# Eight chunks of q and k: rearranged in DRAM and turned in 32x32 blocks on VectorE instead of on TensorE

## The chip, the cores and the metric

The kernel runs on one core of a Trainium2 chip. A core has a TensorE (PE; its weight loads are listed as PEld), a VectorE (DVE), a ScalarE (ACT), a GpSimd (POOL) and a SyncE (SP), which here only issues transfers. Sixteen DMA engines move data between DRAM and the on-chip memory. The engines run side by side and wait for each other by semaphores; each one executes its own instructions in order. The metric is the device time of one execution in microseconds. The profile is of one execution.

## The reference

The program has two parts. The first is linear attention with a decay per head, over 4 sequences (b) of 768 tokens, 8 heads and a head size of 64:

```python
intra = np.einsum('bhic,bhjc->bhij', qb, kb) * Dmask[None]
intra = np.einsum('bhij,bhjd->bhid', intra, vb)
inter = np.einsum('bhid,bhde->bhie', qb * lam_pow[None], kv_state)
out[:, :, sl] = intra + inter
kb_dec = kb * rev_pow[None]
kv_state = lam_block[None, :, None, None] * kv_state + np.einsum('bhsd,bhse->bhde', kb_dec, vb)
```

Its output, seen as 3072 tokens by 512 features, is the x of the second part, a dense mixture of four experts (512 to 1024 to 512):

```python
for e in range(E):
    h = np.maximum(x @ w1[e], 0.0)
    out += p[:, e:e + 1] * (h @ w2[e])
```

Everything is float32.

## The kernel before, in words

**Attention.** The tokens are cut into 24 chunks of 128: chunk n is chunk c = n mod 6 of sequence b = n div 6. A chunk goes through `load` (line 111), `turn` (457), `scores` (480) and `values` (498). `load` brings q, k and v from DRAM into one tile each, with the 128 tokens on the partitions; q and k take two transfers each (for the two halves of the heads), v takes one. `turn` transposes q and k on PE with an identity matrix: four 128x128 transposes each, into the PSUM tiles `qp` and `kp` (line 463). ACT copies those into the tiles `qT` and `kT` (468 and 469), in which the two halves of the head features of a head pair lie on the partitions and the tokens run along the free dimension. For every chunk but the first of a sequence VectorE makes `qs`, q times its decay. For every chunk but the last of a sequence POOL multiplies k, in its untransposed tile, by its decay in place; the transposes read that tile before. `scores` makes the products of k and q (line 486) and has VectorE mask them; `values` makes the outputs and the state, which ACT copies into `xT`.

**Experts.** Eight chunks make a group of 1024 tokens, and there are three groups (g). The x of a group meets four experts in turn; one group with one expert is a unit, and the main loop (line 1193) runs over the twelve units, counted by `at`. Each of the two matrix products of a unit is done by Strassen's scheme with seven products (M1 to M7), and the first one is split by it once more, so its operands are sums of blocks. Those sums are made ahead of time, mostly on POOL, stored to DRAM (`w1_ops`, `x_ops`, `w2_sums`), and loaded again just before use: `feed` (line 659) loads `xs_in` and `ws_in`, one product of the first kind ahead, with two buffers each; `feed2` (764) loads the weights `w2t`, two products ahead. Before the main loop, the first group's product with the first expert is done directly (`direct_product`, line 1045), while the attention of the first group ends.

**The order of the work.** The program is written out by hand: each engine executes in the order in which the code emits. The main loop works on one unit's second product and on the next unit's first product side by side. For each of the seven products (`i`) it has eight slots (`x`), each with a few matmuls of one or of both kinds. Between them it puts:

- `rest()`, which takes one item from a list called `background`: a VectorE operation, for instance a sum for the second product or the masks of `scores`. `soon` puts an attention item at the front of that list.
- steps of the next group's attention: each chunk has three (turn, scores, and values with the load of the chunk two ahead), put in at x = 5, and for i = 1, 3, 5 at x = 2 as well, from the second unit on (line 1258). So a unit takes up to ten steps. Chunks 8 to 15 belong to the units 0 to 2, and chunks 16 to 23 begin in the unit with `at` = 3.
- `pump`, which emits the chores of POOL (the sums for later units, in a first-in first-out list) and the stores of finished sums.

All loads and stores of the main loop go through SP's queue (L123 for q and k, L667 and L669 for `feed`, L775 for `feed2`, L175 to L177 and L248 for stores). An issue there can wait for a buffer to come free, for the data that it stores, or for an earlier transfer, and everything behind it on SP then waits too.

Of the kernel before, what the change touches and what calls it, by code (L numbers as in the profile page):

```python
# [12 lines left out]
ALU = mybir.AluOpType  # L13
# [9 lines left out]
def kernel(  # L23
# [70 lines left out]
    def tt(eng, o, a, b, op):  # L94
        eng.tensor_tensor(out=o, in0=a, in1=b, op=op)  # L95
        if eng is nc.gpsimd:
            busy[0] = max(busy[0], now[0]) + math.prod(o.shape[1:]) / 480
# [13 lines left out]
    def load(n, names="qkv"):  # L111

        b, c = divmod(n, NCH)
        for name in names:
            x = small(f"{name}n")
            src = {"q": q, "k": k, "v": v}[name][b, :, c * C:(c + 1) * C, :]
            if name == "v":
                nc.sync.dma_start(out=x[:].rearrange("p (h d) -> p h d", d=D), in_=src.rearrange("h p d -> p h d"))
            else:
                to, of = x[:].rearrange("p (i r d) -> p i r d", r=2, d=D), src.rearrange("(r i) p d -> p i r d", r=2)  # L120
                for r in range(2):
                    by = nc.scalar if n < 2 and r == 1 else nc.sync
                    by.dma_start(out=to[:, :, r], in_=of[:, :, r])  # L123
            nat[n, name] = x[:].rearrange("p (h d) -> p h d", d=D)
# [219 lines left out]
    def sum_w1(e, name, a, b, op):  # L344
# [6 lines left out]
            tt(nc.gpsimd, to[c], w1_now[e][a][c], w1_now[e][b][c], op)  # L351
        w1_now[e][name] = to

    lam_bc = consts.tile([P, H], FP32, name="lam_bc")
    nc.scalar.dma_start(out=lam_bc[:], in_=lam.partition_broadcast(P))
    for n, names in ((0, "qk"), (1, "qk"), (0, "v"), (2, "qk"), (1, "v"), (3, "qk")):
# [94 lines left out]
    def soon(n, *work):  # L451

        background[0:0] = work
        if n < CPG:
            rest(len(work))

    def turn(n, tags):
        qn, kn = nat.pop((n, "q")), nat[n, "k"]
        qp = bank(tags[0], "qp")
        kp = bank(tags[1], "kp")  # L460
        for x, y in ((qp, qn), (kp, kn)):
            for ac in range(NHP):
                nc.tensor.transpose(  # L463
                    out=x[:, ac * C:(ac + 1) * C], in_=y[:, 2 * ac:2 * ac + 2].rearrange("p r d -> p (r d)"),
                    identity=ident[:],
                )
        qT, kT, qs = small("qT"), small("kT"), None
        nc.scalar.copy(out=qT[:], in_=qp[:])
        nc.scalar.copy(out=kT[:], in_=kp[:])
        if n % NCH:  # L470
            qs = small("qs")
            soon(n, lambda: tt(nc.vector, qs[:], qT[:], q_decay[:].rearrange("p h c -> p (h c)"), ALU.mult))
        turned[n] = qT, kT, qs
        if n % NCH < NCH - 1:

            kd = kn.rearrange("p (ac r) d -> p ac r d", r=2)
            by = k_decay.rearrange("p r ac -> p ac r").unsqueeze(3)
            tt(nc.gpsimd, kd, kd, by.to_broadcast([P, NHP, 2, D]), ALU.mult)

    def scores(n, tags):  # L480
        qT, kT, _ = turned[n]

        sp = [bank(tags[r], "sp") for r in range(2)]
        for ac in range(NHP):
            for r in range(2):
                nc.tensor.matmul(  # L486
                    out=sp[r][:, ac * C:(ac + 1) * C], lhsT=hc(kT)[half[r], ac], rhs=hc(qT)[half[r], ac],
                    start=True, stop=True,
                )
        st = [small("st") for _ in range(2)]  # L490
# [50 lines left out]
    def attention(g):  # L541

        steps = []
        early, late = prepare_x(g)
        for n in range(g * CPG, (g + 1) * CPG):
            steps.append(lambda n=n: turn(n, ("s0", "s1")))
            steps.append(lambda n=n: scores(n, ("s0", "s1")))

            def end(n=n):
                if n == g * CPG:  # L550
                    for m in MS:
                        until(("x", g - 1, m))
# [596 lines left out]
    def sum_own(name, a, b, op=ALU.subtract):  # L1149
# [4 lines left out]
        lambda: own_weights("M1"), sum_own("S1", "A21", "A22", ALU.add), *w2_steps[0:4], mine["M1"], *w2_steps[4:],  # L1154
        raw["A12"],
    ))
    for m in SEQ0[2:]:
        if m == SEQ0[-1]:
            for _ in range(2):
                feed2(*fill2.pop(0))  # L1160
        work = direct_product(0, m, blocks, ("g1", "g3", "q01", "q02", "q11", "q12")) if m != "M5" else [m5[1], *m5[3:]]
        for x, f in enumerate(work):
            f()
            rest()
            if x < len(work) - 1:
                now[0] += 1
                pump(0.75)

    start, w1_steps = now[0], prepare_w1(2)

# [22 lines left out]
    for at, (g, e) in enumerate(units):  # L1193
        if at == 0:
            chores.extend(prepare_w2(2) + prepare_w1(3) + prepare_w2(3) + prepare_w1(0))
        ahead = units[at + 1] if at + 1 < len(units) else None
        nested, nests = g == LAST, ahead and ahead[0] == LAST
        if g == LAST - 1:
            if e == 0:
                chores.append(turn_gates)  # L1200
            chores.extend(prepare_w2_ops(e))
        if ahead and ahead[1] == 0:
            assert not steps
            steps = attention(ahead[0] + 1) if ahead[0] + 1 < NG else []
        blocks, banks = {}, {}
        for i in range(7):
            if fill2:
                feed2(*fill2.pop(0))
            if nested or (nests and i == 6):
                for _ in range(2 if ahead else 16 if i == 0 else 4 if i > 1 else 0):  # L1210
                    if fill3:
                        feed3(*fill3.pop(0))
            if nests and i == 2:
                nc.scalar.dma_start(
                    out=gate_bc, in_=gate_rows[:, ahead[1]].partition_broadcast(P),
                )
            if nested:
                b = nested_product(e, SEQ3[i], (("q01", "q02"), ("q11", "q12"), ("g1", "g3"))[i % (2 if ahead else 3)])
                if i < 6 and (e, SEQ3[i + 1]) != PLAIN:
                    inner_sums(e, SEQ3[i + 1])  # L1220
            else:
                b = second_product(g, e, SEQ2[i], banks)
            if nests and i == 6:
                inner_sums(ahead[1], SEQ3[0], nested)
                if ahead[1] == EARLY[0]:
                    inner_sums(*EARLY, True)
            a = []
            if ahead:
                a = first_product(*ahead, SEQ[i], blocks, ("g1", "g3"))
            if not ahead:  # L1230
                order = [[], b[0:2], [], b[2:4], [], b[4:6], [], b[6:8]]
            elif nested:
                order = [b[0:2], a[0:2], b[2:4], a[2:4], b[4:6], a[4:6], b[6:8], a[6:8]]
            else:
                order = [b[0:1], a[0:2], b[1:2], a[2:4], b[2:3], a[4:6], b[3:5], a[6:8]]
            turned_back = list(after_last.get(SEQ3[i], ())) if nested and not ahead else []
            for x, part in enumerate(order):
                for f in part:
                    if f:
                        f()  # L1240
                now[0] += 1
                if joins:
                    joined()
                elif ahead or x % 2 == 0 and x + i:
                    rest()
                if nested or nests:
                    take(aside)
                if nested and ahead and x in (1, 3) and fill3:
                    feed3(*fill3.pop(0))
                if turned_back and x > 0:  # L1250
                    y = turned_back.pop(0)
                    if y:
# [40 lines left out]
```

## Time and profile before

| | |
|---|---|
| time, median of 9 runs | 1198.38 us (1196.45 to 1199.70) |
| the profiled execution's own time | 1198.89 us |
| its span, first to last instruction | 1197.1 us |
| granted TensorE clock | 1.00 |
| DMA packets | 227991, 317.94 MB |
| DMA packets under 512 B | 91680 |

The profiled execution lasted 1.8 us longer than its span. A line such as `L463` is a line of the kernel; the many sums and products made by the helper `tt` all carry L95. In a group of instructions the form is: line, engine, operation, out<-in by the program's names, partitions x elements, how many; then the busy time in us, the mean of one in ns, and after a second bar the idle time of the engine just before them with what ended it. A wait line reads: engine and line, what it waited for, then the total in us, how often, and the longest. In a timeline the first two numbers are start and duration in us; idle time before is in brackets. In a table of stretches each engine has its busy time in us and its number of instructions, in the order PE, PEld, DVE, ACT, POOL; then come the granted clock, the share of the time in which the 16 DMA engines were busy, and GB/s.

### The profile page before, as it was taken

The page shows a single profiled execution, that of the slowest core. Times are in us where ns is not written, and L with a number is a line of the kernel's source. Part 1 is how long each engine was busy: PE and PEld are TensorE (multiplying, and loading weights), DVE is VectorE, ACT ScalarE, POOL GpSimd, SP SyncE. Part 2 cuts the span into 40 slices and gives each one's busy share as a digit, 9 for nine tenths or more (in the row PEclk, how much of TensorE's full clock was granted, in tenths as well). Part 3 has the DMA queues.
Part 4 walks back from the last instruction along what each step waited for, and adds up shares of the span by engine and source line. Part 5 has one row for each costly group of instructions (what it writes and reads, how often), then busy time and mean ns, then how long its engine had stood idle before and what let it go on. Part 6 is the DMA issues. An engine that isn't in the chain of part 4 may idle for free.

```text
span 1197.1 us, 17886 instructions
## 1 busy us (share of the span) xinstructions
PE 1186.7 (99%) x6623; PEld 1029.9 (86%) x6623; DVE 790.4 (66%) x1318; ACT 261.6 (22%) x478; POOL 635.0 (53%) x600
## 2 busy tenths in 40 slices
PE   9999999999999999999999999999999999999998
PEld 8887888888888888888888888888888888888877
DVE  5597785567467656746754774774665677776784
ACT  3322122112112201311221120120142241240232
POOL 1875248359366800044434745316684683783884
PEclk9999999999999999999999999999999999999999
DMA  9885679999999985689977989898986657566542
GB/s 217 221 295 195 224 261 309 361 318 321 367 344 306 334 274 178 220 287 282 284 275 235 318 298 315 280 313 299 314 285 241 250 193 279 193 251 228 211 167 80
DMA packets 227991, 317.94 MB, mean 266 GB/s; under 512 B 91680, under 2 KB 169408, under 8 KB 227904
## 3 DMA queue, kind: packets, MB, share of 16 engines
q1 hardware_dynamic: 218352, 314.11, 77.5%
q10 hardware_dynamic: 9552, 2.69, 1.1%
q8 instruction: 52, 0.85, 0.3%
q14 instruction: 35, 0.29, 0.1%
HBM read 231.40 MB, written 85.34 MB: 265 GB/s over the span
## 4 chain that ended last, share of the span: by engine, by line
PE 91%; DVE 4%; DMA 2%; POOL 1%; SPq 1%; issue 1%; ACT 0%; ACTq 0%; DVEq 0%; POOLq 0%
PE pg L740 38%; PE q L794 32%; PE pq L966 12%; DVE m L95 2%; PE op L514 2%; PE sp L486 2%; PE pM L1058 1%; PE op L509 1%; PE kp L463 1%; DVE hS L95 1%; SPq L123 1%; PE qp L463 1%; PE op L522 1%; DMA w2b<-in_moe_w_dram 1%; PE pM L936 1%
## 5 line engine op out<-in xcount | busy, mean ns | idle before, releaser
L740 PE MATMUL pg<-xs_in,ws_in 128*128 128x256 f32 x1960 | 470.5, 380 | 1.1 <-DVE m L95 1.0
L740 PEld LDWEIGHTS pg<-xs_in,ws_in 128*128 128x128 f32 x1960 | 370.5, 190 | 54.4 <-DVE m L95 3.6
L95 DVE TENSOR_TENSOR m<-pg,m 128x512 f32<-128x512 f32 x451 | 308.3, 687 | 111.4 <-PE pg L740 102.3
L794 PE MATMUL q<-w2t,hS 128*128 128x256 f32 x1024 | 243.3, 380 | 0.0
L794 PEld LDWEIGHTS q<-w2t,hS 128*128 128x128 f32 x1024 | 192.9, 190 | 26.8 <-issue 0.3
L810 DVE SCALAR_TENSOR_TENSOR acc<-q,gate,acc 128x256 f32<-128x256 f32 x192 | 92.5, 482 | 175.7 <-PE q L794 175.2
L794 PE MATMUL q<-w2t,m 128*128 128x256 f32 x768 | 182.6, 381 | 0.0
L794 PEld LDWEIGHTS q<-w2t,m 128*128 128x128 f32 x768 | 144.6, 190 | 20.4 <-DVE m L95 0.4
L752 ACT ACTIVATE m<-m 128x512 f32<-128x512 f32 x132 | 82.9, 630 | 329.6 <-DVE m L95 321.6
L95 POOL TENSOR_TENSOR m<-m,xT 128x512 f32<-128x512 f32 x64 | 81.6, 1291 | 73.9 <-ACT m L752 56.2
L95 POOL TENSOR_TENSOR kn<-kn,s_decay 128x512 f32<-128x512 f32 x20 | 22.1, 1103 | 164.4 <-PE kp L463 104.0
L95 DVE TENSOR_TENSOR sums<-pq,sums 128x256 f32<-128x256 f32 x154 | 64.5, 421 | 45.9 <-PE pq L966 40.0
L748 ACT COPY m<-pg 128x512 f32<-128x512 f32 x88 | 51.4, 585 | 166.7 <-PE pg L740 161.4
L966 PE MATMUL pq<-acc,w2t 128*128 128x256 f32 x352 | 86.7, 379 | 0.5 <-POOL m L95 0.5
L95 DVE TENSOR_TENSOR m<-m,m 128x512 f32<-128x512 f32 x96 | 81.6, 854 | 0.0
L95 POOL TENSOR_TENSOR ops<-w2b 128x256 f32<-128x256 f32 x24 | 19.7, 840 | 105.3 <-DMA w2b<-in_moe_w_dram 105.3
L966 PEld LDWEIGHTS pq<-acc,w2t 128*128 128x128 f32 x352 | 66.8, 190 | 9.9 <-POOL m L95 0.9
L687 ACT ACTIVATE m<-m 128x512 f32<-128x512 f32 x48 | 30.3, 631 | 154.1 <-DVE m L95 154.1
L95 DVE TENSOR_TENSOR hS<-m,m 128x512 f32<-128x512 f32 x64 | 51.5, 810 | 8.4 <-ACT m L752 8.4
L95 POOL TENSOR_TENSOR acc<-hT,hT 128x512 f32<-128x512 f32 x32 | 40.2, 1272 | 30.1 <-PE pq L966 29.4
L95 POOL TENSOR_TENSOR w2o<-w2b 128x512 f32<-128x512 f32 x32 | 40.5, 1285 | 24.3 <-DMA w2b<-in_moe_w_dram 10.7
L95 POOL TENSOR_TENSOR acc<-hT,acc 128x512 f32<-128x512 f32 x32 | 40.7, 1271 | 7.4 <-PE pq L966 5.4
(131 smaller groups left out, 1323.8 us busy)
## 6 DMA issues: line engine op xcount, KB each, us to landing
xs_in<-x_ops SPq DMA_DIRECT2D x70, 896.0 KB, 5.8
ws_in<-w_ops SPq DMA_DIRECT2D x70, 896.0 KB, 8.7
w2t<-w_ops SPq DMA_DIRECT2D x66, 256.0 KB, 6.7
w2t<-w_sums SPq DMA_DIRECT2D x64, 256.0 KB, 3.9
w_ops<-ops SPq DMA_DIRECT2D x28, 512.0 KB, 6.3
w2t<-in_moe_w_dram SPq DMA_DIRECT2D x48, 256.0 KB, 3.2
x_ops<-ops SPq DMA_DIRECT2D x17, 512.0 KB, 8.6
w2b<-in_moe_w_dram SPq DMA_DIRECT2D x32, 256.0 KB, 6.3
```

The lines of the kernel that those rows point to most:

```text
L95: eng.tensor_tensor(out=o, in0=a, in1=b, op=op)
L123: by.dma_start(out=to[:, :, r], in_=of[:, :, r])
L463: nc.tensor.transpose(out=x[:, ac * C:(ac + 1) * C], in_=y[:, 2 * ac:2 * ac + 2].rearrange("p r d -> p (r d)"), identity=ident[:],)
L486: nc.tensor.matmul(out=sp[r][:, ac * C:(ac + 1) * C], lhsT=hc(kT)[half[r], ac], rhs=hc(qT)[half[r], ac], start=True, stop=True,)
L514: nc.tensor.matmul(out=op[r][half[x], a * C:(a + 1) * C], lhsT=vn[:, 4 * r + 2 * a + x], rhs=hc(st[r])[:, 2 * a + x], start=(first and a = ...
L687: nc.scalar.activation(out=o[:], in_=o[:], func=AF.Relu)
L740: nc.tensor.matmul(out=p[:, j * 256:(j + 1) * 256], lhsT=ws[i][:, j * P:(j + 1) * P], rhs=xs[i], start=(fresh and j == 0), stop=True, skip ...
L748: nc.scalar.copy(out=new[at][:], in_=p[:])
L752: nc.scalar.activation(out=new[at][:], in_=new[at][:], func=AF.Relu)
L794: nc.tensor.matmul(out=p[:, s * DH:(s + 1) * DH], lhsT=h[A_OF[m]][:, c * 256 + s * P:c * 256 + (s + 1) * P], rhs=fed2[g, e, m][uu][:, c], ...
L810: nc.vector.scalar_tensor_tensor(out=o, in0=x, scalar=w, in1=o, op0=ALU.mult, op1=ALU.add)
L966: nc.tensor.matmul(out=p[:, 0:256], lhsT=fed3[e, m, x // 2][:, x % 2, c * P:(c + 1) * P], rhs=b[B_OF[i]][:, c * 256:(c + 1) * 256], start= ...
```

## The change

For the chunks with c = 2 to 5 of the sequences b = 2 and 3, that is the chunks 14 to 17 and 20 to 23, q and k are no longer transposed on PE.

- A DRAM tensor `across` is added. `bring_across(b)` makes 64 KB pieces, 32 for each of the two sequences. A piece copies from q or k, for one head and one half of its features (32 of 64), all 512 tokens from chunk 2 on, in runs of 32 numbers (128 B): `across` then has token mod 32 on the partitions, and a chunk's four 32-token blocks lie side by side in rows of 128 numbers.
- `trickle` issues one piece. For b = 2 pieces are issued after each step of the last two direct products and then at x = 1, 3, 5, 7 of the main loop from its start; for b = 3 they are issued at x = 1, 3, 5, 7 from `at` = 3 on.
- `load_more` replaces `load` at the end of a chunk's values. For a chunk of the eight it issues what is left of the pieces, loads a tile `qx` and a tile `kx` from `across` (512 B runs, one transfer each), and then k and v as before.
- `turn_across` replaces `turn`. It puts three items in front of `background`: `nc.vector.transpose` of `qx` in place, the same of `kx`, and the `qs` product. The 32x32 blocks have been laid out so that the transposed tiles are `qT` and `kT`. The scaling of k on POOL is the same operation as before (now the function `decayed`).
- `scores` takes items from `background` until its chunk is turned.
- In the unit with `at` = 3 the attention steps at x = 2 are left out, so that three of them come later.

```diff
+    ACROSS = {2: 2, 3: 2}
+    across = dram.tile([B, 2, P, NHP, NCH * 4, 32], FP32, name="across")
+    pieces = []
+
+    def bring_across(b):
+        c = ACROSS[b]
+        for x, of in enumerate((q, k)):
+            for y in range(4):
+                for ac in range(NHP):
+                    src = of[b, 4 * (y // 2) + ac, c * C:, (y % 2) * 32:(y % 2 + 1) * 32]
+                    to = across[b, x, y * 32:(y + 1) * 32, ac, c * 4:]
+                    pieces.append(lambda to=to, src=src: nc.sync.dma_start(
+                        out=to, in_=src.rearrange("(t p) d -> p t d", p=32),
+                    ))
+
+    def trickle(m=1):
+        for _ in range(m):
+            if pieces:
+                pieces.pop(0)()
...
+    def load_across(n):
+        b, c = divmod(n, NCH)
+        for x, name in enumerate("qk"):
+            t = small(f"{name}x")
+            nc.sync.dma_start(
+                out=t[:].rearrange("p (h c) -> p h c", c=C),
+                in_=across[b, x, :, :, c * 4:c * 4 + 4].rearrange("p h t d -> p h (t d)"),
+            )
+            nat[n, name + "x"] = t
+
+    def load_more(n):
+        if not comes_across(n):
+            load(n)
+        else:
+            trickle(len(pieces))
+            load_across(n)
+            load(n, "kv")
...
+    def turn_across(n):
+
+        qT, kT, kn = nat.pop((n, "qx")), nat.pop((n, "kx")), nat[n, "k"]
+        qs = small("qs") if n % NCH else None
+
+        def scaled():
+            if n % NCH:
+                tt(nc.vector, qs[:], qT[:], q_decay[:].rearrange("p h c -> p (h c)"), ALU.mult)
+            turned[n] = qT, kT, qs
+
+        soon(n, *(lambda x=x: nc.vector.transpose(out=x[:], in_=x[:]) for x in (qT, kT)), scaled)
+        if n % NCH < NCH - 1:
+            decayed(kn)
+
     def turn(n, tags):
+        if comes_across(n):
+            turn_across(n)
+            return
...
     def scores(n, tags):
+        while n not in turned:
+            rest(force=True)
         qT, kT, _ = turned[n]
...
                 if n + AHEAD < B * NCH:
-                    load(n + AHEAD)
+                    load_more(n + AHEAD)
...
+    bring_across(2)
     for m in SEQ0[2:]:
...
                 pump(0.75)
+            if m in SEQ0[-2:]:
+                trickle()
...
+        if at == 3:
+            bring_across(3)
...
-                if steps and (at > 0 or i > 1) and (x == 5 or (x == 2 and i in (1, 3, 5) and at > 0)):
+                if steps and (at > 0 or i > 1) and (x == 5 or (x == 2 and i in (1, 3, 5) and at not in (0, 3))):
                     steps.pop(0)()
+                if x % 2:
+                    trickle()
                 pump(PACE[g])
```

More of the change, by code (lines that the diff above doesn't have):

```diff
@@ L352, in sum_w1, with comes_across @@
         w1_now[e][name] = to
+    ACROSS = {2: 2, 3: 2}
[15 more added lines that the diff above has]
+                pieces.pop(0)()
+    def comes_across(n):
+        b, c = divmod(n, NCH)
+        return b in ACROSS and c >= ACROSS[b]
+    def load_across(n):
+        b, c = divmod(n, NCH)
+        for x, name in enumerate("qk"):
[12 more added lines that the diff above has]
+            load(n, "kv")
     lam_bc = consts.tile([P, H], FP32, name="lam_bc")
@@ L455, in soon, with decayed @@
             rest(len(work))
+    def decayed(kn):
+        kd = kn.rearrange("p (ac r) d -> p ac r d", r=2)
+        by = k_decay.rearrange("p r ac -> p ac r").unsqueeze(3)
+        tt(nc.gpsimd, kd, kd, by.to_broadcast([P, NHP, 2, D]), ALU.mult)
+    def turn_across(n):
[8 more added lines that the diff above has]
+            decayed(kn)
     def turn(n, tags):
+        if comes_across(n):
+            turn_across(n)
+            return
         qn, kn = nat.pop((n, "q")), nat[n, "k"]
@@ L474, in turn @@
         if n % NCH < NCH - 1:
-            kd = kn.rearrange("p (ac r) d -> p ac r d", r=2)
-            by = k_decay.rearrange("p r ac -> p ac r").unsqueeze(3)
-            tt(nc.gpsimd, kd, kd, by.to_broadcast([P, NHP, 2, D]), ALU.mult)
+            decayed(kn)
     def scores(n, tags):
+        while n not in turned:
+            rest(force=True)
         qT, kT, _ = turned[n]
```

## The prediction

> **What bounds the kernel now.** I read the page's busy shares and TensorE clock first, then who waits for whom on PE, then busy time by stretch, and last the instructions around one turn. From the page:
>
> ```profile
> PE 1186.7 (99%) x6623; PEld 1029.9 (86%) x6623; DVE 790.4 (66%) x1318; ACT 261.6 (22%) x478; POOL 635.0 (53%) x600
> PEclk9999999999999999999999999999999999999999
> ...
> q1 hardware_dynamic: 218352, 314.11, 77.5%
> q10 hardware_dynamic: 9552, 2.69, 1.1%
> ```
>
> PE is busy for 1186.7 of 1197.1 us at the full granted clock. A modelled end can flatter that, so the waits decide; between 100 and 640 us PE waited twice:
>
> ```profile
> PE pg L740 <- DVE m L95: 1.0, 2, 0.6
> ```
>
> With 1.0 us of waits in 540 us, PE is the bound where the change acts: work taken off PE shortens the kernel, and anything else costs only once it makes PE wait. Busy time of all engines in five stretches (the last two numbers of a line are the DMA share and GB/s):
>
> ```profile
> 63.00:103.00 40.00, 38.85 (x178) 33.29 (x178) 39.66 (x57) 9.00 (x16) 25.36 (x20) 1.00 0.64 225
> 103.00:175.00 72.00, 71.45 (x387) 62.23 (x386) 55.39 (x95) 12.64 (x22) 26.28 (x28) 1.00 0.71 247
> 287.00:398.00 111.00, 110.50 (x690) 95.25 (x689) 72.11 (x115) 21.32 (x39) 69.13 (x68) 1.00 0.98 332
> 398.00:502.00 104.00, 104.00 (x614) 90.03 (x614) 64.50 (x107) 21.13 (x39) 19.68 (x22) 1.00 0.76 253
> 502.00:640.00 138.00, 138.00 (x857) 119.41 (x856) 79.31 (x136) 27.76 (x53) 59.69 (x68) 1.00 0.83 268
> ```
>
> **What it removes: 64 transposes on PE.** Eight chunks (14 to 17, 20 to 23) lose four qp and four kp transposes each. Rows of all 24 chunks, by shape, and one turn in the timeline:
>
> ```profile
> L463 PE MATMUL qp<-ident,qn 128*128 128x128 f32 x96 | 15.0, 280 | 0.5 <-DMA qn<-in_q_dram 0.5
> L463 PE MATMUL kp<-ident,kn 128*128 128x128 f32 x96 | 14.8, 277 | 0.3 <-DMA kn<-in_k_dram 0.3
> ```
>
> ```profile
> 335.73 0.60 PE L463 MATMUL qp<-ident,qn 128*128 128x128 f32 x4
> ...
> 336.16 0.60 PE L463 MATMUL kp<-ident,kn 128*128 128x128 f32 x4
> ...
> 336.60 1.89 PE L794 MATMUL q<-w2t,hS 128*128 128x256 f32 x8
> ```
>
> The mean of 280 ns is no price, because transposes overlap: the eight start at 335.73 and the next work at 336.60, so a turn holds PE for 0.87 us. Eight turns: 8 x 0.87 = **7.0 us**. The 16 copies on ACT go too (591 ns for the kT one); ACT is busy for 21 of 104 us here and no PE wait names it, so they count nothing.
>
> **What it adds on VectorE: 16 transposes, 128x512 in place.** No such row exists. Bounds: half the tile copied from PSUM (kv<-op, 128x256, 420 ns) below; the longest qs<-qT,q_decay (1469 ns) above. I take 0.69 us, the median of that product: same tile, same pool, in the same place. That is 11 us on an engine idle for 39 of 111 us (287 to 398) and 59 of 138 us (502 to 640). They go through the background list, at most one item a slot of about 1.73 us of PE, as the 0.8 us hS sums do; a chunk takes two more slots. By my count of the slots one sum is forced out early, at chunk 23, and at chunks 22 and 23 the sp products follow the k transpose by a slot only: there PE's whole queue stands behind a wait on VectorE instead of ACT. I put 0.4 us of new PE waits on this (half of one 0.69 us item); without idle slots each item would hold up an accumulator's eviction.
>
> The Trainium skill (VectorE: DVE Perf Modes, The three transpose paths) gives 311 ns for a 128x128 bf16 transpose on VectorE; four of those make 1.24 us, an estimate, so 20 us by the page against 11. Both fit in the idle time, and no row here shows which holds for fp32.
>
> **What it adds on the queues: 64 rearranging transfers.** Each moves 64 KB from DRAM to DRAM in 512 runs of 128 B, 32 runs for each of 16 engines. The page has 1.1% x 16 x 1197 / 9552 = 22 ns a packet on q10 (mean 282 B) and 77.5% x 16 x 1197 / 218352 = 68 ns on q1 (mean 1439 B). A line through both gives 11 ns plus 0.040 ns a byte: 16 ns at 128 B, 0.51 us of all engines a piece. Ends: 11 ns (the bare intercept) and 68 ns (q1's mean, nearer if a DRAM write of 128 B is dear); I take 16, since q10's small packets are the nearest row.
>
> - First stretch: ten pieces during the last two direct products, 22 in the first unit. SP runs ahead, so pieces start near 63 us, where the queue is full: five stand before the w2t loads issued at 65.22, and eight before the w_sums store at 69.68, for which POOL idles until 75.71. That is 5 x 0.51 = 2.6 us on w2t, which is first used more than 20 us after its issue, and 8 x 0.51 = 4.1 us on POOL, whose operands of that time PE reads from 107 us on; POOL's last of them ends at 96.7 and it then waits 8.98 us for PE anyway. Engines free until 175: 36% of 40 plus 29% of 72 = 35 us, against 32 x 0.51 = 16. Counted nothing.
> - Second stretch (fourth unit, 398 to 502, and the next product): 28 pieces x 0.51 = 14 us against 24% of 104 = 25 us free. Each product's pieces come after its xs_in and ws_in loads, which have a product (about 14 us) to land and take 5.8 and 8.8 us there. Cover: 5 us. Without it every further us is a PE wait.
> - SP: 64 issues at the 0.5 us of a q load, four to a product of 14 us; SP itself waits 23 us for PE at L775 in this stretch. The loads of a turned chunk remain five issues: two of 512 B runs for the two halves of q. By the line 2 x 32 x 31 - 64 x 21 ns = 0.65 us more of the engines a chunk. Nothing.
> - Chunk 20's load waits for the landing of the last pieces, with the next product's loads queued behind it; pieces are issued at least 5 us earlier and transfers land in 3 to 9 us here, so up to 4 us of SP, inside the cover.
>
> The Trainium skill (DMA: Bandwidth & Descriptors, Specifications) says that a transfer below 512 B is done as a read-modify-write, which speaks against this change. Taken as twice my price, an estimate, a piece costs 1.0 us and the second stretch 28.7 against 25 free; the 3.7 over lies inside the 5 us, so the sum stays. No write below 512 B is in this trace.
>
> **What it moves.** The scaling of k on POOL waits no longer for PE's transposes:
>
> ```profile
> POOL kn L95 <- PE kp L463: 92.2, 9, 28.7
> ```
>
> ```profile
> 368.01 1.06 POOL L95 TENSOR_TENSOR kn<-kn,s_decay 128x512 f32<-128x512 f32 x1 [9.97 <-issue]
> ...
> 385.92 1.27 POOL L95 TENSOR_TENSOR xo<-xT 128x512 f32<-128x512 f32 x1
> ```
>
> This matters at one place. After chunk 15's scaling at 368.01 POOL runs without a break into the sums of the second group (385.92), their stores, and the loads:
>
> ```profile
> 405.85 0.32 SPq L667 DMA_DIRECT2D xs_in<-x_ops  x1
> 406.22 0.42 SPq L669 DMA_DIRECT2D ws_in<-w_ops  x1
> ```
>
> ```profile
> 415.58 1.75 PE L740 MATMUL pg<-xs_in,ws_in 128*128 128x256 f32 x7
> ```
>
> 406.22 plus 8.8 is 415.0: hardly any slack. PE now comes 2 x 0.87 = 1.7 us earlier. If POOL's chain stayed, 1.7 us would be lost; but its 9.97 us idle time before 368.01 falls away, so the sums start when xT is ready, some 1.7 us earlier plus what POOL was late, and I count nothing (bounds 0 and 1.7). Three steps of attention leave the fourth unit, so that PE, ACT and VectorE do the same work later, the loads of chunks 18 and 19 (ten issues on SP) come one and two products later, and the second group's attention and POOL's sums behind it end two products (26 us) later. Chunk 18 is still loaded two products ahead of its turn; the sums' operands land by 737 and the first is loaded at 785, which hides it; else up to 14 us would be lost.
>
> **The sum.** The profiled execution took 1198.89 us (span 1197.1 and 1.8 around it): 1198.89 - 7.0 + 0.4 = 1192.3. It stands 0.5 over the median of 1198.38; against that, **1191.8**, with a range of its own of 1190.3 to 1193.5.
>
> **Rivals.**
> 1. Slower: dear small packets in the second stretch. From 25 / 28 = 0.89 us a piece (28 ns a packet) loads fall late; with 5 us of cover and 7 us of gain the kernel stops being faster at 37 / 28 = 1.3 us (41 ns). At 55 ns, between that and q1's 68: 28 x 1.76 = 49, less 25 and 5, is 19 us of PE waits: 1198.4 - 7 + 19 = 1210. For: no such transfer has a row, and queues are at 0.9 and more in the first half. Against: packets of 282 B on average go at 22 ns.
> 2. VectorE late: at 1.47 us a transpose, each in the way of an eviction with about 1 us to spare, 16 x 0.47 = 7.5 us come back: 1198.9. For: sums of SBUF tiles reach 1.4 us beside POOL. Against: a third of VectorE is idle.
> 3. A part of the gain hidden: the operand chain at 415 keeps 1.7 us and the pieces push one more tight load back by 1 to 2: 1195. For: the slack of that chain. Against: POOL's earlier start.
>
> That the transposes stay on PE is excluded by the code: those chunks issue none.
>
> **How the numbers follow.** Likeliest 0.64; rival 3 0.13; rival 2 0.08; rival 1 0.13; more than 7.5 us gained 0.02. The range 1190.0 to 1197.0 takes in the first two and the upper bound of rival 3 and leaves out about 0.2. This kernel can tell about 0.2% (2.4 us) from no change: faster 0.64 + 0.13 + 0.02 = 0.79, same 0.08, slower 0.13.
>
> **What the changed profile would show.** L463 on PE x128 instead of x192; 16 new DVE transposes near 0.7 us; PE waits between 100 and 640 still near 1 us; DMA share in the fourth unit 0.85 to 0.95; no POOL wait on kp for the eight chunks. Wrong if PE shows waits of several us on xs_in or ws_in between 400 and 520, packets of the pieces cost over 28 ns, or the PE waits on DVE grow past 3 us.

## The result, and the profile after

The changed kernel takes 1193.87 us (median of 10 runs, 1191.91 to 1195.75), against a forecast of 1191.8 and a range of 1190.0 to 1197.0. Its ratio to the kernel before is 0.9963, with a 95% interval of 0.9955 to 0.9971: it is faster by 4.4 us (3.5 to 5.4), where 6.6 were forecast. The profiled execution took 1193.08 us, with a span of 1191.3.

From the page of the changed kernel, busy shares, clock and the two DMA queues:

```profile
PE 1179.5 (99%) x6559; PEld 1023.2 (86%) x6559; DVE 807.7 (68%) x1334; ACT 253.1 (21%) x462; POOL 634.2 (53%) x600
PEclk9999999999999999999999999999999999999999
...
q1 hardware_dynamic: 252144, 320.40, 80.9%
q10 hardware_dynamic: 9552, 2.69, 1.1%
```

TensorE has the 64 transposes less (6559 instead of 6623 instructions) and 7.2 us less work. The added VectorE transposes, and what is left of the transposes on PE, as groups by shape:

```profile
L530 PE MATMUL qp<-ident,qn 128*128 128x128 f32 x64 | 10.2, 284 | 0.0
L530 PE MATMUL kp<-ident,kn 128*128 128x128 f32 x64 | 9.7, 275 | 0.0
L517 DVE STREAM_TRANSPOSE qx<-qx 128x512 f32<-128x512 f32 x8 | 5.6, 701 | 0.0
L517 DVE STREAM_TRANSPOSE kx<-kx 128x512 f32<-128x512 f32 x8 | 5.5, 690 | 0.0
```

Busy time in the five stretches of the prediction (same columns):

```profile
63.00:103.00 40.00, 37.55 (x171) 31.85 (x170) 39.69 (x54) 8.96 (x15) 24.82 (x20) 1.00 0.79 238
103.00:175.00 72.00, 70.86 (x384) 61.69 (x384) 55.69 (x96) 12.17 (x22) 25.36 (x28) 1.00 0.81 256
287.00:398.00 111.00, 111.00 (x686) 96.14 (x686) 77.68 (x120) 19.15 (x36) 69.33 (x70) 1.00 0.99 342
398.00:502.00 104.00, 104.00 (x568) 90.09 (x567) 70.17 (x115) 20.26 (x36) 20.52 (x21) 1.00 0.87 273
502.00:640.00 138.00, 138.00 (x831) 119.42 (x831) 85.99 (x142) 22.16 (x40) 61.67 (x70) 1.00 0.94 299
```

The chunks with the new turns lie in the last three, and there PE is busy all the time. The first two are the ones that got worse: PE loses 1.3 us more than before in 63 to 103 (2.45 idle against 1.15) and 0.6 more in 103 to 175. In the first of them VectorE is busy for 39.69 of 40 us, and makes 54 operations in the time in which it made 57.

When the two traces are laid over each other matmul by matmul, the changed kernel falls behind by 0.38, 0.48, 0.59 and 0.70 us at four places between 93 and 105 us, 2.15 us together, and then gains 0.87 us at each turn that is gone. (At 23 us, 40 us before the first piece, the profiled execution of the changed kernel is already 1.2 us ahead; the profiled executions of the experiments stand between 1.2 us ahead and 1.0 us behind there. So the two profiles lie 5.8 us apart where the medians differ by 4.4, and losses are read from the steps, not from absolute times.) Who PE waited for from 84 to 108 us, before:

```profile
PE pg L740 <- DVE m L95: 1.3, 2, 0.7
PE pg L740 <- POOL ops L95: 0.4, 1, 0.4
```

and after:

```profile
PE pg L806 <- DVE m L95: 2.7, 3, 1.1
PE pg L806 <- ACT m L814: 0.9, 1, 0.9
```

So the loss is VectorE being late, and VectorE had no new work there. Its sums of two SBUF tiles (SBUF is the on-chip memory that holds the tiles; matmuls write into PSUM) are longer. The hS<-m,m group of VectorE between 88 and 104 us, before and then after:

```profile
L95 DVE TENSOR_TENSOR hS<-m,m 128x512 f32<-128x512 f32 x4 | 2.7, 676 | 0.0
```

```profile
L95 DVE TENSOR_TENSOR hS<-m,m 128x512 f32<-128x512 f32 x4 | 4.3, 1084 | 0.0
```

These four are 1.6 us longer in all; the first 0.38 us are lost ahead of them, among VectorE's sums before 93 us. What changed beside them is POOL. Issues on SP and sums on POOL in the timeline, before:

```profile
69.68 0.41 SPq L248 DMA_DIRECT2D w_sums<-w2o  x1
...
75.71 2.53 POOL L95 TENSOR_TENSOR w2o<-w2b 128x512 f32<-128x512 f32 x2 [7.11 <-DMA w_sums<-w2o]
```

and after:

```profile
66.17 2.18 SPq L367 DMA_DIRECT2D across<-in_q_dram  x2
...
68.40 2.44 SPq L841 DMA_DIRECT2D w2t<-in_moe_w_dram  x4
70.88 0.56 SPq L367 DMA_DIRECT2D across<-in_q_dram  x1
71.54 1.08 SPq L240 DMA_DIRECT2D w2b<-in_moe_w_dram  x2
72.66 1.24 SPq L367 DMA_DIRECT2D across<-in_q_dram  x2
74.00 1.08 SPq L248 DMA_DIRECT2D w_sums<-w2o  x1
...
79.10 2.97 POOL L95 TENSOR_TENSOR w2o<-w2b 128x512 f32<-128x512 f32 x2 [11.60 <-DMA w_sums<-w2o]
```

The store that POOL waits for is issued 4.3 us later, and POOL's idle time grows from 7.11 to 11.60 us. POOL's chain of sums then ends at 100.2 instead of 96.7 us. Before, two of the four hS sums came after that end; now all four lie beside POOL's sums. Sums of this length are not new: in the kernel before, those beside POOL's sums from 79 to 86 us take 1.16 to 1.21 us each. The delay moves the overlap to later sums, close to where PE waits for VectorE.

### The profile page after: what moved, and what is told of

Its sections match the earlier page's. It is cut to its first block, busy times and chain, and to the rows that moved or that the text cites. A ratio compares the mean times of both kernels' runs of the same rounds, so it can differ in the third digit from the quotient of the medians.

```text
span 1191.3 us, 17827 instructions
## 1 busy us (share of the span) xinstructions
PE 1179.5 (99%) x6559; PEld 1023.2 (86%) x6559; DVE 807.7 (68%) x1334; ACT 253.1 (21%) x462; POOL 634.2 (53%) x600
## 4 chain that ended last, share of the span: by engine, by line
PE 88%; DVE 6%; DMA 2%; POOL 2%; issue 1%; ACT 0%; SPq 0%; ACTq 0%; DVEq 0%; POOLq 0%
PE pg L806 36%; PE q L860 30%; PE pq L1032 12%; DVE m L95 2%; PE sp L552 2%; PE op L580 2%; PE pM L1124 1%; DVE hS L95 1%; DMA w_ops<-w2o 1%; PE op L575 1%; DMA ws_in<-w_ops 1%; PE op L588 1%; DVE xt L95 1%; PE qp L530 1%; DMA w_ops<-ops 1%
## 5 line engine op out<-in xcount | busy, mean ns | idle before, releaser
L95 DVE TENSOR_TENSOR hS<-m,m 128x512 f32<-128x512 f32 x64 | 56.1, 882 | 4.9 <-ACT m L818 4.9
```

## The experiments

The theory to begin with: the pieces of the first stretch hold the w_sums store up, POOL's sums come 4.5 us later, they meet VectorE's sums where VectorE is the bound, and PE waits for VectorE. The rivals: the small packets themselves cost something wherever they are; or a turn is worth less than 0.87 us.

**1. The pieces of the first stretch later.**

```diff
-            if m in SEQ0[-2:]:
-                trickle()
...
-                if x % 2:
+                if 2 <= i <= 5 if at == 0 else x % 2:
                     trickle()
```

> The changed kernel with one thing moved: the 32 pieces of the first stretch are issued one a slot in the products i = 2 to 5 of the first unit (about 127 to 165 us) and none earlier. Theory (the early pieces hold the w_sums store up, POOL's sums come 4.6 us later and then run beside VectorE, whose sums go from 0.68 to 1.2 us where VectorE is the bound, 84 to 108 us): the PE waits on VectorE there go, 2.2 us come back, median near 1191.7, ratio to before 0.9944; hS sums at 93 to 100 us at 0.68 us again. Rival (the turns give less than 0.87 us each and the first stretch is innocent; what the traces show at 84 to 108 us is the jitter of single runs): the time stays at 1193.9, ratio 0.9963. A third case (the pieces cost whatever they are beside): the waits turn up again at 127 to 165 us as waits on operand loads, 1193 to 1195.

Measured: 1192.22 us, ratio 0.9952 (0.9939 to 0.9964). The hS sums and PE's waits on VectorE from 84 to 108 us:

```profile
L95 DVE TENSOR_TENSOR hS<-m,m 128x512 f32<-128x512 f32 x4 | 2.7, 678 | 0.0
```

```profile
PE pg L806 <- DVE m L95: 1.6, 2, 1.0
```

The same 32 pieces, 60 us later, leave the sums at 0.68 us, and 1.65 of the 2.1 us that the forecast missed come back. The intervals of this version and of the changed kernel overlap, so the times alone do not part them; the rows do. It is the fastest version found here, level with number 4.

**2. The first pieces alone, in the kernel before.** `bring_across(2)` and the two `trickle` calls of the first stretch are added to the kernel before, and nothing else.

```diff
+    bring_across(2)
     for m in SEQ0[2:]:
...
+            if m in SEQ0[-2:]:
+                trickle()
...
+                if x % 2:
+                    trickle()
                 pump(PACE[g])
```

> The kernel before with nothing added but the 32 pieces of the first stretch, in the places of the changed kernel; nothing reads what they write. Theory (they hold up POOL and so slow VectorE at 84 to 108 us): 2.2 to 2.9 us slower than before, 1200.6 to 1201.3, ratio 1.0018 to 1.0024, with POOL's first w2o sum at about 79 instead of 75.7 us. Rival (pieces are free there, the gain of the turns is smaller): 1198.4, ratio 1.0000.

Measured: 1199.93 us, ratio 1.0014 (1.0005 to 1.0022): 1.7 us (0.6 to 2.6) slower, where 2.2 to 2.9 were expected by the theory and nothing by the rival. POOL's idle time before its w2o sum was 12.1 us, and the four hS sums took 0.97 us on average. Number 1 takes the cost away, number 2 makes it alone.

**3. One sequence.**

```diff
-    ACROSS = {2: 2, 3: 2}
+    ACROSS = {3: 2}
...
-    bring_across(2)
...
-            if m in SEQ0[-2:]:
-                trickle()
```

> The changed kernel with the sequence b = 3 alone: four chunks (20 to 23) turned on VectorE, the pieces of the second stretch only, and the attention steps of the fourth unit moved as in the changed kernel. Theory (a turn on PE costs 0.87 us and the second stretch, the transposes and the moved steps are free): 4 x 0.87 = 3.5 us, 1194.9, ratio 0.9971, and no new PE waits at 84 to 108 us. Rival (the second stretch or the moved steps cost 1 us or more): 1196 or above, ratio 0.9980 or more. If a turn were worth only half, 1196.6.

Measured: 1195.35 us, ratio 0.9977 (0.9968 to 0.9986): 2.8 us (1.7 to 3.8) for four turns. The expected 3.5 lies in the interval; a turn of half the worth (1.7) is at its edge. POOL's idle time was 7.0 us, the hS sums took 0.68 us.

**4. The same pieces behind the store.**

```diff
-            if m in SEQ0[-2:]:
+            if m == SEQ0[-1] and x > 2:
                 trickle()
```

> The changed kernel with the first pieces put behind the w_sums store that POOL waits for: the eight positions ahead of it issue nothing, two pieces follow it among the direct products, and the other 30 at x = 1, 3, 5, 7 of the main loop. The same 32 pieces and bytes, moved by about 15 us at the most. Theory (the order on SP decides: store late, POOL late, VectorE slowed): POOL starts its w2o sum near 75.7 us again and most of the 2.2 us comes back, 1191.7 to 1192.4. Rival (the 128 B packets as such slow the queues or the tiles' owners in this stretch, whatever stands first): no more than half comes back, 1192.8 to 1193.9.

Measured: 1192.35 us, ratio 0.9950 (0.9938 to 0.9963), with the store issued at 69.81 us, POOL's idle time at 6.5 us and the hS sums at 0.68 us. PE's waits on VectorE from 84 to 108 us have not gone, though:

```profile
PE pg L806 <- DVE m L95: 2.3, 2, 1.8
```

Laid over the kernel before, this run loses 1.07 us there, half of what the changed kernel lost, with VectorE behind already at 85 us. Its PE was 1.0 us ahead at 60 us, so its POOL, starting at 75.93 us, is still 1.2 us late against the rest. The pieces may run in this stretch, as long as they do not stand ahead of that one store: by the time, nearly nothing is lost then.

**5. An eighth of each piece.** Added to the kernel before, as in number 2; each piece copies 64 tokens of 512.

```diff
-                    src = of[b, 4 * (y // 2) + ac, c * C:, (y % 2) * 32:(y % 2 + 1) * 32]
-                    to = across[b, x, y * 32:(y + 1) * 32, ac, c * 4:]
+                    src = of[b, 4 * (y // 2) + ac, c * C:c * C + 64, (y % 2) * 32:(y % 2 + 1) * 32]
+                    to = across[b, x, y * 32:(y + 1) * 32, ac, c * 4:c * 4 + 2]
```

> The kernel before with the 32 pieces of the first stretch in their places, each cut to an eighth: 64 runs of 128 B instead of 512, so nearly the same issues on SP (0.55 to 0.7 us each) and an eighth of the transfer. Nothing reads what they write. Theory (what holds the w_sums store up is the time that the pieces take of the 16 DMA engines, about 0.4 us each by the spacing of their landings): POOL starts its w2o sum at 76 us or earlier than 76.5, no more than 0.3 us is lost, 1198.4 to 1198.7. Rival (the issues on SP hold the store up, eight at 0.55 to 0.7 us ahead of it): the store is issued 4 us later as with the full pieces, POOL starts near 80 us and the 1.5 us of the full pieces is lost again, 1199.9.

Measured: 1199.53 us, ratio 1.0010 (1.0001 to 1.0020). My theory fell. From its timeline and its waits (POOL, 60 to 110 us):

```profile
65.51 2.77 SPq L365 DMA_DIRECT2D across<-in_q_dram  x4
...
73.54 0.53 SPq L248 DMA_DIRECT2D w_sums<-w2o  x1
```

```profile
POOL w2o L95 <- DMA w_sums<-w2o: 10.9, 1, 10.9
```

With an eighth of the bytes the store is still issued at 73.54 us, POOL still idles for 10.9 us, and PE's waits from 84 to 108 us (3.1 us on VectorE, 0.9 on ScalarE) are no shorter than in the changed kernel; the four hS sums took 1.09 us on average. SP issues one transfer after the other there, 0.56 to 0.69 us for each piece, so eight of them ahead of the store take some 5 us of SP whatever they carry. What the pieces cost in this stretch is places in SP's queue, not time of the DMA engines.

**6. Three pieces at each place of the second stretch.** On top of number 1; the 64 extra pieces go to a DRAM tensor that nothing reads.

```diff
+    spare = dram.tile([2, B, 2, P, NHP, NCH * 4, 32], FP32, name="spare")
...
             bring_across(3)
+            bring_across(3, spare[0])
+            bring_across(3, spare[1])
...
-                    trickle()
+                    trickle(3 if at else 1)
```

> The version with the first stretch later (1192.2 us), with three pieces instead of one at each place of the second stretch: 64 more pieces from 398 us on, into a DRAM tensor that nothing reads. Theory (0.41 us of all engines a piece; 13 us of the fourth unit are left free at a share of 0.87, and about 5 us of cover): 64 x 0.41 = 26 us, less 13.5, 1 and 5, about 6 us of PE waits on ws_in or xs_in, near 1198; with the 0.51 us of the prediction 12 us, 1204. Rival (the queue has much more room than the share says, or a piece costs 0.25 us or less): no loss, 1192 to 1193.

Measured: 1224.72 us, ratio 1.0218 (1.0204 to 1.0232), 32.5 us above number 1: five times what I expected. PE's waits from 398 to 530 us, and the fourth unit by busy time, here and then in number 1:

```profile
PE pg L807 <- DMA ws_in<-w_ops: 19.0, 5, 7.8
```

```profile
398.00:502.00 104.00, 90.96 (x482) 77.03 (x481) 57.96 (x95) 14.24 (x25) 17.58 (x18) 0.93 0.85 240
```

```profile
398.00:502.00 104.00, 103.55 (x566) 89.78 (x565) 68.41 (x113) 19.14 (x34) 16.16 (x17) 1.00 0.85 262
```

The share of the DMA engines is 0.85 in both, so it is not the engines that fill up. An added piece occupies SP for a median of 0.63 us and for up to 3.3; why some take so long the profile does not say. Three at a place make 12 a product, and they can fill nearly all of its 14 us:

```profile
461.38 12.05 SPq L368 DMA_DIRECT2D spare<-in_q_dram  x12
```

The ws_in load behind them is then issued too late. The rest of the loss stands in the clock: 0.93 of full speed.

**7. Each block transpose three times.** On top of number 1.

```diff
-        soon(n, *(lambda x=x: nc.vector.transpose(out=x[:], in_=x[:]) for x in (qT, kT)), scaled)
+        soon(n, *(lambda x=x: [nc.vector.transpose(out=x[:], in_=x[:]) for _ in range(3)] for x in (qT, kT)), scaled)
```

> The version with the first stretch later (1192.2 us), with each block transpose on VectorE made three times in a row, in place, as one item of the background list: the result is the same, each item lasts 2.1 us instead of 0.70, 32 transposes or 22 us more on VectorE. Theory (a third of VectorE is idle and accumulators have time): at most two items reach the end, at chunks 22 and 23, 1192 to 1195. Rival (each item stands in the way of an eviction with about 1 us to spare, as the rival of the prediction reckoned): 16 x 1.1 us, near 1209, with as many PE waits on m.

Measured: 1206.49 us, ratio 1.0068 (1.0054 to 1.0081), 14.3 us above number 1, or 0.9 us for each item that became 1.4 us longer. PE's waits from 300 to 720 us:

```profile
PE pg L806 <- DVE m L95: 4.8, 9, 0.7
PE sp L552 <- DVE kx L517: 4.8, 2, 2.8
```

This is near the rival's 17 us. An idle third of VectorE is no room for an item of 2.1 us: most of each one's extra time arrives at the end. The two waits of the sp products on kx, which the prediction expected at chunks 22 and 23, are here; in the changed kernel, at 0.69 us a transpose, PE never waits on kx.

**8. The moved steps alone**, in the kernel before.

```diff
-                if steps and (at > 0 or i > 1) and (x == 5 or (x == 2 and i in (1, 3, 5) and at > 0)):
+                if steps and (at > 0 or i > 1) and (x == 5 or (x == 2 and i in (1, 3, 5) and at not in (0, 3))):
```

> The kernel before with nothing changed but the attention steps at x = 2, which are left out of the fourth unit, so that three steps come later; all turns stay on PE. The version with one sequence gained 2.8 to 3.0 us where four turns are worth 3.5. Theory (moving the steps costs the missing half us, by VectorE's sums meeting POOL's at other places): 1198.8 to 1199.3, ratio 1.0003 to 1.0008. Rival (the move is free and the half us is lost at the transposes or the pieces): 1198.4, ratio 1.0000. Were the move itself a gain, it would be below 1198, and part of the changed kernel's gain would be its.

Measured: 1199.13 us, ratio 1.0002 (0.9994 to 1.0011). This settles nothing within 1 us. Its trace has one PE wait of 0.5 us on VectorE between 640 and 720 us that the kernel before lacks, and so have the changed kernel and numbers 1 and 3.

**9. Two more chunks.** On top of number 1.

```diff
-    ACROSS = {2: 2, 3: 2}
+    ACROSS = {2: 0, 3: 2}
```

> The version with the first stretch later (1192.2 us), with the whole of sequence 2 brought across: chunks 12 and 13 too are turned on VectorE, ten chunks in all, and the 32 pieces of the first stretch carry 768 tokens instead of 512. Theory (a turn is worth 0.87 us of PE wherever the queue has room): 2 x 0.87 = 1.7 us less, 1190.5, ratio 0.9937. Rival (at 193 to 287 us the DMA engines are busy to 0.95 and more, and each of the chunks loads a 256 KB tile kx more): ws_in comes late there, PE waits of 1 us or more on it, 1192 or above.

Measured: 1194.63 us, ratio 0.9964 (0.9950 to 0.9977). Laid over number 1, the two turns do gain 0.83 and 0.88 us, but before that one wait loses more. PE's waits from 108 to 398 us, and the matmuls from 256 to 262 us by shape:

```profile
PE pg L806 <- DMA ws_in<-w_ops: 4.4, 1, 4.4
```

```profile
L806 PE MATMUL pg<-xs_in,ws_in 128*128 128x256 f32 x8 | 3.7, 647 | 4.4 <-DMA ws_in<-w_ops 4.4
L860 PE MATMUL q<-w2t,m 128*128 128x256 f32 x5 | 2.3, 631 | 0.0
```

The load of chunk 12 stands ahead of that ws_in load and is one tile larger; SP reaches the ws_in issue at 245.3 instead of 239.1 us. After the wait the matmuls last 0.65 us instead of the 0.38 that they take at the full clock, and PE loses another 2.9 us before it is back at speed. The trace is of the slowest of six executions (1190.87 to 1196.83 us). The fastest is where the theory had it, so whether the wait comes each time is not known.

**10. The steps back, six pieces a product.** On top of number 1.

```diff
-                if 2 <= i <= 5 if at == 0 else x % 2:
+                if 2 <= i <= 5 if at == 0 else x not in (0, 7):
                     trickle()
...
-                if steps and (at > 0 or i > 1) and (x == 5 or (x == 2 and i in (1, 3, 5) and at not in (0, 3))):
+                if steps and (at > 0 or i > 1) and (x == 5 or (x == 2 and i in (1, 3, 5) and at > 0)):
```

> The version with the first stretch later (1192.2 us), with the attention steps at x = 2 put back into the fourth unit, and the pieces of the second stretch issued six to a product instead of four, since chunk 20 is then loaded a product earlier. Theory (the move costs 0.4 us, the PE wait of 0.5 us on m at 640 to 720 that came with it, and SP has room for six pieces a product): 1191.5 to 1192.2. Rival (SP is full with six pieces, 6 x 0.62 = 3.7 us a product more): operand loads are late in the fourth unit, PE waits on ws_in, 1194 or above.

Measured: 1197.44 us, ratio 0.9991 (0.9982 to 1.0000). Nearly the whole gain is gone (eleven executions from 1193.67 to 1200.74), and PE's one wait from 398 to 502 us says where the rival was right:

```profile
PE pg L806 <- DMA ws_in<-w_ops: 3.8, 1, 3.8
```

The fourth unit has room on SP for four pieces a product, and not for six together with the loads of chunks that come earlier; which of the two fills it was not separated.

**11. The first pieces on ScalarE's queue.**

```diff
-                    pieces.append(lambda to=to, src=src: nc.sync.dma_start(
+                    pieces.append(lambda to=to, src=src: (nc.scalar if b == 2 else nc.sync).dma_start(
```

> The changed kernel with the 32 pieces of the first stretch in their old places but issued from ScalarE's queue instead of SP's. Theory (what held the w_sums store up is the eight issues ahead of it on SP): the store is issued near 69.7 us again, POOL starts before 77, and most of the 1.6 us comes back, 1192.2 to 1192.9, if ScalarE's copies don't suffer from its 32 issues. Rival (the transfers themselves, by their share of the 16 engines): the store is issued in time but lands as late as in the changed kernel, POOL starts at 79, 1193.9. Against both: an issue of 0.6 us or more in ScalarE's way delays its copies of pM and m, and PE waits on ACT, 1194 to 1197.

Measured: 1195.08 us, ratio 0.9973 (0.9963 to 0.9982), with PE waits on VectorE of 3.8 us from 84 us on, the longest 2.6, and one of 1.6 on ScalarE. ScalarE did not get to its first piece before 80.8 us, and yet SP issued the store only at 73.10. SP's waits from 62 to 79 us:

```profile
SPq L240 <- DMA w2b<-in_moe_w_dram: 2.9, 2, 2.6
```

SP stood for 2.6 us until an earlier w2b load had landed, which it does not in the kernel before. By the semaphore numbers in the trace, the transfers of both queues share eight of them in turn, so each piece in the code brings the next use of a semaphore forward for SP, even if it is issued elsewhere. That explanation was not tried by itself. What the run adds: POOL was late (start at 78.4 us) with no piece yet under way. PE lost 3.7 us in the same place, but not by POOL's delay alone: ScalarE's operation at 88.08 us had waited 2.7 us for one of the pieces, and PE's 1.6 us at 98.01 us ended on a copy of ScalarE that stood among its issues, which is the expectation's third case.

**12. The w2t loads behind the store.** On top of number 1, with nothing added.

```diff
     for m in SEQ0[2:]:
-        if m == SEQ0[-1]:
-            for _ in range(2):
-                feed2(*fill2.pop(0))
...
                 pump(0.75)
+            if m == SEQ0[-1] and x == 3:
+                for _ in range(2):
+                    feed2(*fill2.pop(0))
```

> The version with the first stretch later (1192.2 us), with nothing added and one thing moved: the four w2t loads that stand ahead of the w_sums store on SP (issued at 65 to 67 us) are issued right after it. Theory (the order on SP sets when POOL's sums run, and those that run beside VectorE's sums at 88 to 100 us slow it): the store lands up to 3 us earlier, POOL starts its w2o sum at 72 to 74.5 instead of 75.2, is done by 94 instead of 96, VectorE's ops and hS sums there get shorter, the 2.0 us of PE waits at 84 to 108 us fall to 0.5 to 1.5, and the time is 1190.7 to 1191.7. Rival (the loss of the changed kernel is bound to the pieces themselves, not to when POOL runs): POOL starts earlier and nothing comes of it, 1192.2. Against both: w2t is late for the product at 93 us, PE waits on it, 1193 or above.

Measured: 1193.76 us, ratio 0.9959 (0.9945 to 0.9972); expected was a gain. POOL's idle time fell to 3.85 us and it started at 74.3 us, as the theory said, but laid over number 1 this run loses about 1.8 us from 78 to 104 us. VectorE in the timeline, here and then in number 1:

```profile
72.11 1.88 DVE L95 TENSOR_TENSOR m<-pM,m 128x512 f32<-128x512 f32 x3
73.91 5.70 DVE L95 TENSOR_TENSOR m<-m,m 128x512 f32<-128x512 f32 x4
79.54 1.87 DVE L95 TENSOR_TENSOR m<-pM,m 128x512 f32<-128x512 f32 x3
```

```profile
70.89 1.88 DVE L95 TENSOR_TENSOR m<-pM,m 128x512 f32<-128x512 f32 x3
72.68 2.49 DVE L95 TENSOR_TENSOR m<-m,m 128x512 f32<-128x512 f32 x4
75.09 2.48 DVE L95 TENSOR_TENSOR m<-pM,m 128x512 f32<-128x512 f32 x4
```

Four sums of SBUF tiles took 2.49 us as long as POOL was idle, and 5.70 with POOL's sums (from 74.3 us) beside three of them: 1.75 us each. The operations that read PSUM (pM) take the same 0.6 us a piece in both. So "POOL later is bad" was too simple. What counts is which sums of two SBUF tiles POOL meets, and in this stretch, where VectorE has no slack, a shift of POOL in either direction cost something.

## Why the prediction was right or wrong

- **Turns off PE, 8 x 0.87 = 7.0 us: right.** Where the traces of before and number 1 are laid over each other, the six that stand apart from the moved steps show as steps of 0.87 or 0.88 us each.
- **VectorE's transposes at 0.69 us: right** (0.70 and 0.69), by the nearest row. The estimate of 1.24 us from the Trainium skill (VectorE: DVE Perf Modes, The three transpose paths) was not borne out for fp32. How much hung on this number, the prediction did not say: number 7 shows that 1.4 us more on each would have cost more than the gain.
- **0.4 us of new PE waits at chunks 22 and 23: wrong in place.** PE never waits on kx. Instead there are 0.5 us on VectorE at 640 to 720 us, which the moved steps bring without any transpose (number 8), and 0.3 us on ws_in at 252 us.
- **A piece at 0.51 us of all engines: a little dear.** The 32768 packets of 128 B in the changed kernel's trace took 12.9 ns each, against 16 in the prediction, so a piece costs 0.41 us; the fourth unit's share, up from 0.76 to 0.87, says the same: 0.11 x 104 / 28 = 0.41. The alternative of 1.0 us a piece is out. The prediction's sentence that the trace before has no write below 512 B cannot be meant of all writes, since that kernel's table counts 91680 packets below 512 B. Rival 1, dear packets, is out: the time is far from 1210, and no PE wait on ws_in or xs_in falls between 398 and 520 us.
- **"First stretch ... Counted nothing": this step failed.** Its first half came out right in size: POOL late by 4.1 us was forecast, and its idle time grew by 4.5. Its second half asked only when PE reads what POOL makes (from 107 us on). It did not ask what runs beside POOL at its new time. VectorE does, at 39.66 of 40 us in the prediction's own table, and its sums grew from 0.68 to 1.08 us on average. The price is 1.65 us by number 1 and 1.7 by number 2, most of the 2.1 us by which the forecast was off. The prediction had the means: its second rival says that "sums of SBUF tiles reach 1.4 us beside POOL". The reason for the delay was wrong too: it was eight issues on SP, not eight transfers (number 5), so that the size came out was luck. Number 11 shows that the store can also be late without these issues.
- **Second stretch, counted nothing: right, by the wrong bound.** No PE wait fell there. But the cover was not 25 us of free engines, as the prediction had it; it was SP's idle time. Four pieces a product fit into it and twelve do not (number 6); six together with the earlier chunk loads did not either (number 10).
- **The operand chain at 415 us and chunk 20's load, counted nothing: right.** PE does not wait in the fourth unit. POOL no longer waits for PE's transposes of the eight chunks; its waits on kp from 300 to 640 us fell from 78.7 us in seven to the two of chunks 18 and 19:

```profile
POOL kn L95 <- PE kp L530: 14.4, 2, 7.2
```

- **The moved steps, free: not refuted** (0.2 us, with an interval from -0.7 to 1.3).
- **Rivals.** The third, a part of the gain hidden (1195), came nearest in size, but neither of its places was the one. The second, VectorE late through the transposes, did not come at 0.69 us each; number 7 shows that it does at 2.1.

The 0.4 us that number 1 leaves between forecast and measurement is within what these runs can tell.

## What to carry to other kernels

Where a change delays an engine that has slack, ask what runs beside it at its new time, and not only who waits for its results: here 4.5 us of delay on an engine with 9 us of slack cost 1.7 us through a neighbour without any. Count added transfers as places in the issuing queue first, at about 0.6 us each here and in front of whatever follows them, and only then as bytes or engine time. Before placing added transfers, look for the one store or load behind them that somebody is already waiting for; putting the pieces behind that store gave the same time as moving them away altogether (numbers 4 and 1).

## What the hardware showed that was not expected

- **VectorE beside POOL.** A sum of two 128x512 SBUF tiles takes 0.68 us alone and 1.08 on average (0.82 to 1.21) beside POOL's sums in the changed kernel; three in a row took 1.75 us each in number 12. With one operand in PSUM no such sum (m<-pM,m and m<-pg,m) takes more than 0.69 us in any of the traces. The Trainium skill (SBUF — State Buffer, Who interferes with whom) says just this: a VectorE instruction with two SBUF inputs contends with a GpSimd instruction that reads SBUF, and one with at most one SBUF input does not, outside the modes that use both ports; the order of issue decides which of the two is blocked. The traces agree. In the kernel before an hS sum that began at 94.23 us, 0.15 us ahead of a POOL sum, took its 0.68 us, and POOL's took 1.12 instead of 0.79; in the changed kernel one that began at 95.07, 0.6 us before the end of a POOL sum, took 1.16. The prediction did not use this rule.
- **The clock after a wait.** In number 9 a PE wait of 4.4 us was followed by matmuls at 0.65 instead of 0.38 us, and the wait cost 7 us in all; in number 12 a wait of 2.0 us was followed by a clock of 0.89 from 92 to 98 us, which is half speed for 3.41 us:

```profile
92.00:98.00 6.00, 4.02 (x15) 2.80 (x15) 5.93 (x10) 1.52 (x3) 3.14 (x4) 0.89 0.42 169
96.65:100.06 3.41, 3.41 (x8) 2.73 (x9) 3.38 (x7) 2.12 (x4) 0.00 (x0) 0.50 0.63 251
```

  Not every wait of this length does it. In number 11 one of 2.6 us ended at 107.8 us, and the clock stayed:

```profile
108.00:114.00 6.00, 6.00 (x29) 5.28 (x29) 3.91 (x6) 1.76 (x3) 5.76 (x7) 1.00 1.07 313
```

  In number 7 it stayed after a wait of 2.0 us and fell after one of 2.8. Waits of up to 1.1 us in the changed kernel and of 1.8 in number 4 show no such effect. The Trainium skill (TensorE: Matmul & The Clock Gate, Part 1) has the clock fall after an idle window of about 3.4 us; numbers 7 and 12 show it after shorter waits.
- **Small packets.** A packet of 128 B from DRAM to DRAM took 12.9 ns in the changed kernel's trace, or 0.41 us of all engines for a piece of 512: no more than the line through the two queues had said (0.51).
